# Batch 2's transposed q and k copied out by ScalarE and VectorE, its first k through another PSUM bank, its q and k loaded in halves of four heads

## The chip, the cores and the metric

The kernel runs on one core of one Trainium2 chip. The metric is the device time of one execution in microseconds (us). The kernel before takes 345.33 us, the median of three runs (345.21 to 345.88).

The engines are named as in the profile: PE is TensorE, PEld its weight loads, DVE is VectorE, ACT is ScalarE, POOL is GpSimd, SP is SyncE. Each engine works through its own queue in order. L254 is line 254 of the kernel before.

## The reference, cut to what matters

Inputs are `q`, `k`, `v` of 8 batches x 8 heads x 576 positions x 64, forget factors `f` of 8 x 8 x 576, and two weight matrices (512 x 2048 and 2048 x 512). For each batch and head a causal attention with decay is computed, and its output, 4608 tokens by 512, goes through a small MLP:

```
scores = q k^T / 8 + cum[i] - cum[j]        # cum = cumsum(log(clip(f, 1e-4, 1)))
attn   = softmax over j <= i
x      = (attn v), heads side by side       # 4608 x 512
h      = x w_in;  g = h - tanh(h);  out = g w_out
```

## The kernel before

Work is in fp16 with fp32 sums in PSUM. Heads are taken in pairs, four pairs to a batch. For the scores of a head both q and k must lie with the 64 head dimensions on the partitions (`QT` and `KT`, two buffers each, used by even and odd batches). How they get there depends on the batch. Batch 0 is turned by PE in blocks. **Batches 1 and 2** are loaded by POOL's DMA queue (`load_qk`, L213, with a cast from fp32 to fp16) and turned by PE, one pair at a time, in `trans` (L245). Batches 3 to 7 (`FAR = 3`) are turned by DMA.

`trans(b, c, src, dst, eng)` turns q or k of pair `c` of batch `b`: six PE transposes (L254) into one PSUM bank, then two copies to SBUF, one from partitions 0 to 63 into the even positions, one from partitions 64 to 127 into the odd ones. The two letters of `eng` name the engine of each copy: A is ACT (L261), V is DVE (L263).

The bank comes from a pool. `ps_tr` has one bank; `ps_m` has three, used in turn, and is shared with the MLP: a bank holds one tile of the first MLP product (`hps`, L448 or L462) until its gate is done, or one output tile of the second (`ops`, L581). `ps_sc` has two banks for scores (`ps`, L358), `ps_av` two for the attention output (`av`, L386).

The order on every engine is the order in which the program is written out (`manual_schedule`). The main loop is `slot(p, take)`, p = 4 to 32, one slot for each head pair from batch 1 on (p = 4 is batch 1's first pair, p = 8 batch 2's first). In slot p seven score tiles are emitted, each with its exponential on ACT (`e`, L367) and, from the second pair on, a causal mask on POOL (L377). Among them, by score tile number `ti`, come the loads listed in `LOADS`, the `values` of the pair before (L386, then three DVE operations L392 to L394), and the two `trans` calls for the next pair: q at `ti` 0 and k at `ti` 3, but at 2 and 4 in slot 7, which prepares batch 2's first pair. So batch 2 is turned in slots 7, 8, 9 and 10. Between these items MLP steps are spread: `mlp1` makes an `hps` tile, ACT takes its tanh (`th`, L414) and DVE adds it (`gt`, L415); `mlp2` adds four products to `ops` and copies it out on ACT (L585). `TAKE` says how many steps a slot gets: 5 in slot 7, 7 in slot 8, 9 in slot 9, 8 in slot 10.

The loads of batch 2's q and k are issued in slot 4, behind four loads of `wout` (L210), one DMA for all 8 heads of q at `ti` 5 and one for k at `ti` 6. POOL then issues, in the slots after, batch 2's v (L95, five DMAs in slot 6) and batch 3's q and k by heads (L106). Eight completion semaphores are used in turn by POOL's DMAs; a DMA waits until the one eight before it on the same semaphore has landed.

Of the kernel before, what the change touches and what calls it, by code (L numbers as in the profile page):

```python
# [22 lines left out]
def kernel(  # L23
# [13 lines left out]
    B, H, S, D = q.shape  # L37
# [4 lines left out]
    NPAIR = H // 2  # L42
# [34 lines left out]
    HH = H // 2  # L77
    raw = [[qkp.tile([P, RW], FP16, tag=f"{x}n{i}", name=f"{x}n{i}") for i in range(2)] for x in "qk"]
    qn, kn = ([t[0:S // NT6, :].rearrange("p (h n d) -> p h n d", h=H, n=NT6) for t in ts] for ts in raw)
# [8 lines left out]
    QT = [qkp.tile([D + 3, H, S], FP16, tag=f"QT{i}", name=f"QT{i}") for i in range(2)]  # L88
    KT = [qkp.tile([D + 3, H, PITCH], FP16, tag=f"KT{i}", name=f"KT{i}") for i in range(2)]
# [12 lines left out]
    def load_heads(dst, src, b, n):  # L102
        pn = min(P, S - n * P)
        to = dst[0:pn, n * P:n * P + D]
        to = bass.AP(to.tensor, to.offset, [list(to.ap[0]), [HP, H], [1, D]])
        nc.gpsimd.dma_start(out=to, in_=src[b, :, n * P:n * P + pn, :].rearrange("h p d -> p h d"))  # L106

    def turn_all(dst, src):
        nc.sync.dma_start_transpose(out=dst.rearrange("p (x t) -> p x t", t=P), in_=src[:, 0:TC])
# [5 lines left out]
    def load_v(b, n):  # L115
        load_block(vn[b % 2], v, b, n)

    def raw_of(b):
        return 1 if b == FAR else 0
# [48 lines left out]
    def load_aug(b):  # L168
        i, h0 = b % 2, b * H
        nc.sync.dma_start(out=KT[i][D:D + 1, :, 0:S], in_=chi[h0:h0 + H, :])  # L170
        nc.sync.dma_start(out=QT[i][D + 2:D + 3, :, :], in_=cq[h0:h0 + H, :])
        nc.sync.dma_start(out=KT[i][D + 1:D + 2, :, 0:S], in_=clo[h0:h0 + H, :])
# [40 lines left out]
    def load_qk(dst, src, b, h0, h1):  # L213
        nc.gpsimd.dma_start(
            out=dst[b % 2][:, h0:h1, :, :].rearrange("p h n d -> p h (n d)"),
            in_=src[b, h0:h1, :, :].rearrange("h (p n) d -> p h (n d)", n=NT6))

    LOADS = {(NPAIR, 5): [lambda: load_qk(qn, q, 2, 0, H)],
             (NPAIR, 6): [lambda: load_qk(kn, k, 2, 0, H)]}
    for i in range(2 * HF):  # L220
        LOADS.setdefault((2 * NPAIR + 3 + i // 4, i % 4 * 2), []).append(lambda i=i: weight_sums(i))
    for b in range(2, B):
        p0 = (b - 1) * NPAIR
        for n in range(NJ):
            LOADS.setdefault((p0 + (2 if b == 2 else 1), n), []).append(lambda b=b, n=n: load_v(b, n))
        LOADS.setdefault((p0, 0), []).append(lambda b=b: load_aug(b))
        if b < FAR:
            continue
        for n in range(NJ):
            LOADS.setdefault((p0 - 1, n), []).append(lambda b=b, n=n: load_heads(raw[0][raw_of(b)], q, b, n))  # L230
            LOADS.setdefault((p0, n), []).append(lambda b=b, n=n: load_heads(raw[1][raw_of(b)], k, b, n))
        LOADS.setdefault((p0, 4), []).append(lambda b=b: turn_all(TQ, raw[0][raw_of(b)]))
        LOADS.setdefault((p0 + 1, 4), []).append(lambda b=b: turn_all(TK, raw[1][raw_of(b)]))
# [4 lines left out]
    E, XN, GT, M2, AV = {}, {}, {}, {}, {}  # L238
# [5 lines left out]

    def trans(b, c, src, dst, eng):  # L245
        pn, g3 = S // NT6, NT6 // 2
        if b == 1 and src is kn:
            t32 = ps_m.tile([P, UW], FP32, tag="m", name="t32")
        else:
            t32 = ps_tr.tile([P, UW], FP32, tag="tr", name="t32")  # L250
        t16 = t32.bitcast(FP16)[:, 0:2 * S // 2].rearrange("p (a g n) -> p a g n", a=2, g=g3)
        for a in range(2):
            for g in range(g3):
                nc.tensor.transpose(out=t16[:, a, g, :],  # L254
                                    in_=src[b % 2][:, 2 * c + a, 2 * g:2 * g + 2, :],
                                    identity=id16[0:pn, 0:pn])
        for e in range(2):
            to = dst[b % 2][0:D, 2 * c:2 * c + 2, e:S:2].rearrange("d a (p g) -> d a p g", g=g3)
            of = t16[e * D:(e + 1) * D, :, :, :].rearrange("d a g p -> d a p g")
            if eng[e] == "A":  # L260
                nc.scalar.activation(out=to, in_=of, func=AF.Copy)  # L261
            else:
                nc.vector.tensor_copy(out=to, in_=of)  # L263
# [83 lines left out]
    def scores(b, c, ti):  # L347
        ps = ps_sc.tile([P, 512], FP32, tag="sc", name="ps")
        if ti == LAST:
            e = EL[(b * NPAIR + c) % 3]  # L350
        else:
            e = aex.tile([P, 512], FP16, tag="e", name="e")
        lo = min(x[4] for x in TILES[ti])
        hi = max(x[4] + x[3] for x in TILES[ti])
        for a, j, i0, n, col in TILES[ti]:
            h = 2 * c + a
            edge = min(P, n) if (b, c) == (1, 0) and i0 == j * P else 0
            nc.tensor.matmul(out=ps[:, col:col + n], lhsT=KT[b % 2][0:D + 3, h, j * P:(j + 1) * P],  # L358
                             rhs=QT[b % 2][0:D + 3, h, i0:i0 + n], start=True, stop=not edge)
            if edge:  # L360
                nc.tensor.matmul(out=ps[:, col:col + edge], lhsT=neg16, rhs=tri16[:, 0:edge],
                                 start=False, stop=True)
            for ib in range(j, NJ):
                w0 = min(ib * P, S - P)
                if i0 <= ib * P < i0 + n:
                    E[(b, h, j, ib)] = e[:, col + w0 - i0:col + w0 - i0 + P]
        nc.scalar.activation(out=e[:, lo:hi], in_=ps[:, lo:hi], func=AF.Exp, scale=qscale)  # L367
        if (b, c) == (1, 0):
            return
        col, cp, step, wd = MASKS[ti]  # L370
        view = e[:, col:col + (cp - 1) * step + wd]
        if cp == 1:
            pat = [[1, wd]]
        else:
            view = bass.AP(view.tensor, view.offset, [list(view.ap[0]), [step, cp], [1, wd]])
            pat = [[0, cp], [1, wd]]
        nc.gpsimd.affine_select(out=view, in_=view, compare_op=ALU.is_ge, fill=0.0,  # L377
                                base=0, pattern=pat, channel_multiplier=-1)
# [19 lines left out]
    def turn(b, c):  # L398
        xn = XN.pop((b, c))
        r0 = b % RB * S  # L400
        nc.sync.dma_start_transpose(out=XR[:, c, r0:r0 + S - D].rearrange("p (n t) -> p n t", t=P),
                                    in_=xn[:, 0:NJ - 1, :].rearrange("p n d -> p (n d)"))
        nc.sync.dma_start_transpose(out=XR[:, c, r0 + S - D:r0 + S], in_=xn[D:P, NJ - 1, :])
# [27 lines left out]
    def weight_sums(i):  # L431
        what, x = divmod(i, HF // 2)
        lo, hi = slice(2 * x, 2 * x + 2), slice(HF + 2 * x, HF + 2 * x + 2)
        b11, b12, b21, b22 = (wout[:, r, c] for r in (lo, hi) for c in (slice(0, HD), slice(HD, DM)))
        t2x = t2[x // 2][:, x % 2 * 2:x % 2 * 2 + 2, :]
        out, in0, in1 = ((t1[:, lo, :], b12, b11), (t2x, b22, t1[:, lo, :]),
                         (t3[:, lo, :], b22, b12), (tn4[:, lo, :], b21, t2x))[what]
        nc.vector.tensor_tensor(out=out, in0=in0, in1=in1, op=ALU.subtract)
# [167 lines left out]
    def att_items(p):  # L606
        items = []
        here = pairs[p] if p < len(pairs) else None
        before = pairs[p - 1] if NPAIR < p else None
        after = pairs[p + 1] if p + 1 < len(pairs) else None  # L610
        for ti in range(len(TILES)):
            if here:
                items.append((lambda ti=ti: scores(*here, ti), "s%d" % ti))
            for load in LOADS.get((p, ti), ()):
                items.append((load, ""))
            late = 2 * (p == 2 * NPAIR - 1)
            if ti == late and after and after[0] < FAR:
                items.append((lambda: trans(*after, qn, QT, "AV" if after[0] == 1 else "VV"), "q"))
            if ti == 1 and before:
                items.append((lambda: (values(*before), turn(*before)), "v"))  # L620
            if ti == 3 + late // 2 and after and after[0] < FAR:
                items.append((lambda: trans(*after, kn, KT, "VV"), "k"))
        return items

    goal = [0]
# [114 lines left out]
    scores0(4, 3)  # L740
    step()
    trans(1, 0, qn, QT, "AV")
    scores0(4, 4)
    turn0(3)
# [40 lines left out]
```

## Time and profile before

| what | value |
|---|---|
| median of 3 runs | 345.33 us (345.21 to 345.88) |
| profiled execution: time, and span of the core | 346.0 us, 344.3 us |
| granted TensorE clock | 1.00 |
| busy PE, DVE, ACT, POOL | 334.6, 236.2, 222.9, 158.6 us |
| PE transposes L254 (batches 1 and 2) | 96, 203 to 208 ns each |
| copies L263 on DVE | 27, 783 to 815 ns each |
| copies L261 on ACT | 5, 806 to 829 ns each |
| stretch 58 to 62 us, busy PE | 1.88 + 1.31 of 4.00 us |
| stretch 76 to 92 us, busy PE, DVE, ACT | 15.76, 13.81, 12.38 of 16.00 us |
| stretch 120 to 300 us, busy PE | 180.00 of 180.00 us |

The span is the time between the first and the last instruction on the core; the profiled time lies 1.7 us above it. A busy time adds up the durations of an engine's instructions. PE's instructions are pipelined, so the start of one matmul after the start of another tells more of PE's pace than their durations do.

### The profile page before, as it was taken

What the parts mean: (1) busy time and instruction counts of PE and PEld (TensorE: products, weight loads), DVE (VectorE), ACT (ScalarE), POOL (GpSimd) and SP (SyncE); (2) the same over time, 40 slices, a digit from 0 to 9 for tenths busy, and PEclk for the clock granted to TensorE, in tenths of its full rate; (3) what the DMA queues carried; (4) which work ended last, traced back from release to release, by engine and by line L of the source; (5) the groups of instructions that cost most, each with busy time, mean ns of one, the idle gap of its engine ahead of it and who ended that gap; (6) DMA issues with size and microseconds to landing.
All of it is one profiled execution on the core that took longest, in us unless ns stands there. A gap on an engine that the chain in (4) does not pass through costs nothing.

```text
span 344.3 us, 8688 instructions
## 1 busy us (share of the span) xinstructions
PE 334.6 (97%) x3354; PEld 235.2 (68%) x3354; DVE 236.2 (69%) x481; ACT 222.9 (65%) x417; POOL 158.6 (46%) x318
## 2 busy tenths in 40 slices
PE   7989999999999999999999999999999999999995
PEld 3879875655455557888886568656887786486485
DVE  6496886658953598558764895478637865975973
ACT  4677976558755786578757875687568844623631
POOL 8966448755267726664586548652222210000000
PEclk9999999999999999999999999999999999999999
DMA  9999999999799999999999999999330013002002
GB/s 88 140 197 188 204 203 141 169 159 233 126 141 127 202 175 151 123 193 184 164 145 188 172 159 181 182 172 184 91 110 19 17 50 109 3 30 93 0 32 91
DMA packets 161323, 45.96 MB, mean 134 GB/s; under 512 B 141506, under 2 KB 159234, under 8 KB 161282
## 3 DMA queue, kind: packets, MB, share of 16 engines
q0 software_dynamic: 100128, 18.36, 74.8%
q1 hardware_dynamic: 61074, 26.99, 39.8%
q8 instruction: 26, 0.43, 0.6%
q14 instruction: 15, 0.12, 0.1%
q10 hardware_dynamic: 80, 0.07, 0.1%
HBM read 36.85 MB, written 9.44 MB: 134 GB/s over the span
## 4 chain that ended last, share of the span: by engine, by line
PE 88%; DVE 5%; ACT 4%; POOL 1%; issue 1%; DMA 1%; ACTq 0%; DVEq 0%
PE hps L462 31%; PE cx L503 14%; PE cz L503 11%; PE ps L358 10%; PE ops L581 7%; PE av L386 7%; PE hps L448 2%; PE ps L300 2%; DVE gt L415 1%; PE t L272 1%; ACT e L305 1%; DVE QT L263 1%; ACT e L367 1%; ACT th L414 1%; PE av L313 1%
## 5 line engine op out<-in xcount | busy, mean ns | idle before, releaser
L415 DVE TENSOR_TENSOR gt<-hps,th 128x512 f16<-128x512 f32 x144 | 98.4, 688 | 42.7 <-ACT th L414 41.6
L462 PE MATMUL hps<-XR,win 128*128 128x512 f16 (+4 forms) x640 | 125.7, 336 | 0.2 <-DVE gt L415 0.2
L367 ACT ACTIVATE e<-ps 128x512 f16<-128x512 f32 x168 | 98.5, 594 | 37.4 <-PE ps L358 34.7
L414 ACT ACTIVATE th<-hps 128x512 f32<-128x512 f32 x144 | 86.1, 598 | 29.5 <-PE hps L462 19.8
L377 POOL TENSOR_SCALAR_AFFINE_SELECT e<-e 128x128 f16<-128x128 f16 x162 | 55.3, 342 | 105.9 <-ACT e L367 105.6
L462 PEld LDWEIGHTS <-win 128*128 128x128 f16 x640 | 56.3, 97 | 43.7 <-issue 0.5
L358 PE MATMUL ps<-QT,KT 67*128 67x512 f16 (+1 forms) x336 | 68.7, 277 | 0.5 <-DVE KT L263 0.3
L503 PEld LDWEIGHTS <-gt 128*128 128x128 f16 x560 | 52.5, 97 | 8.2 <-DVE gt L415 0.4
L358 PEld LDWEIGHTS <-KT 67*128 67x128 f16 x336 | 31.9, 98 | 21.7 <-DVE KT L263 0.8
L95 POOL DMA_DIRECT2D vn<-in_v_dram x40 | 34.2, 859 | 5.9 <-DMA win<-in_moe_w_in_dram 3.0
L581 PE MATMUL ops<-wout,gt 128*128 128x512 f16 x128 | 32.6, 378 | 0.0
L386 PEld LDWEIGHTS <-e 128*128 128x128 f16 x784 | 28.1, 97 | 3.3
L496 DVE TENSOR_TENSOR snap<-cz,snap 128x512 f32<-128x512 f32 x21 | 14.5, 691 | 22.4 <-PE cz L503 7.4
L386 PE MATMUL av<-vn,e 128*128 128x65 f16 x784 | 29.2, 193 | 0.0
L503 PE MATMUL cz<-wout,gt 128*128 128x256 f16 x224 | 27.8, 272 | 0.0
L394 DVE TENSOR_TENSOR xn<-av,rs 128x640 f16<-128x640 f32 x28 | 23.1, 825 | 1.0
L503 PEld LDWEIGHTS <-sw 128*128 128x128 f16 x224 | 21.1, 97 | 3.9
L106 POOL DMA_DIRECT2D qn<-in_q_dram x25 | 21.3, 852 | 1.7 <-issue 1.7
L106 POOL DMA_DIRECT2D kn<-in_k_dram x25 | 21.3, 853 | 1.2 <-issue 1.2
L540 ACT ACTIVATE snap<-cx 128x512 f32<-128x512 f32 (+1 forms) x16 | 8.7, 544 | 16.2 <-PE cx L503 16.2
L581 PEld LDWEIGHTS <-gt 128*128 128x128 f16 x128 | 11.2, 97 | 9.8
L305 ACT ACTIVATE e<-ps 128x512 f16<-128x512 f32 x25 | 14.3, 596 | 4.9 <-PE ps L303 2.9
(108 smaller groups left out, 377.4 us busy)
## 6 DMA issues: line engine op xcount, KB each, us to landing
vn<-in_v_dram POOLq DMA_DIRECT2D x32, 128.0 KB, 6.7
out_dram<-ost SPq DMA_DIRECT2D x14, 256.0 KB
out_dram<-snap SPq DMA_DIRECT2D x14, 256.0 KB
qn<-in_q_dram POOLq DMA_DIRECT2D x24, 128.0 KB, 5.3
kn<-in_k_dram POOLq DMA_DIRECT2D x24, 128.0 KB, 4.5
QT<-TQ SPq DMA_DIRECT2D x10, 288.0 KB
KT<-TK SPq DMA_DIRECT2D x10, 288.0 KB
win<-in_moe_w_in_dram POOLq DMA_DIRECT2D x2, 1024.0 KB, 12.1
```

The costliest lines, as they stand in the source:

```text
L95: nc.gpsimd.dma_start(out=dst[0:pn, n, h0:h1, 0:D], in_=src[b, h0:h1, n * P:n * P + pn, :].rearrange("h p d -> p h d"))
L106: nc.gpsimd.dma_start(out=to, in_=src[b, :, n * P:n * P + pn, :].rearrange("h p d -> p h d"))
L358: nc.tensor.matmul(out=ps[:, col:col + n], lhsT=KT[b % 2][0:D + 3, h, j * P:(j + 1) * P], rhs=QT[b % 2][0:D + 3, h, i0:i0 + n], start=True ...
L367: nc.scalar.activation(out=e[:, lo:hi], in_=ps[:, lo:hi], func=AF.Exp, scale=qscale)
L377: nc.gpsimd.affine_select(out=view, in_=view, compare_op=ALU.is_ge, fill=0.0, base=0, pattern=pat, channel_multiplier=-1)
L386: nc.tensor.matmul(out=av[:, a, ib, :], lhsT=E.pop((b, 2 * c + a, j, ib)), rhs=vn[b % 2][:, j, 2 * c + a, 0:D + 1], start=(j == 0), stop=( ...
L394: nc.vector.tensor_tensor(out=xn.rearrange("p i (a d) -> p a i d", a=2), in0=av[:, :, :, 0:D], in1=rs.to_broadcast([P, 2, NJ, D]), op=ALU. ...
L414: nc.scalar.activation(out=th, in_=hps, func=AF.Tanh, scale=-1.0)
L415: nc.vector.tensor_tensor(out=to, in0=view(hps), in1=view(th), op=ALU.add)
L462: nc.tensor.matmul(out=hps[:, o:o + n], lhsT=win[:, ci, ft * P:(ft + 1) * P], rhs=XR[:, ci, t:t + n], start=(ci == 0), stop=(ci == NCH - 1))
L503: nc.tensor.matmul(out=ps, lhsT=stationary(u, LHS[ph], ft, m), rhs=moving(RHS[ph], ft), start=fresh and ft == 0, stop=(ft == HF - 1), skip ...
L581: nc.tensor.matmul(out=ops, lhsT=GT[(u, ft, m)], rhs=wout[:, ft, :], start=(ft == 0), stop=(ft == NFT - 1))
```

## The change

Three things are done, all for batch 2 alone. In `trans`, the two copies of each of its eight transposed tiles (q and k of four pairs) go to ACT and DVE, where both went to DVE; batch 1's stay as they are (q by ACT and DVE; k by DVE alone but for its first pair). The k tile of batch 2's first pair takes a bank of `ps_m` where it took the bank of `ps_tr`; batch 1's k did so before. And batch 2's q and k are loaded in four DMAs, four heads each, in the order q low, k low, q high, k high, where they were loaded in two.

```diff
-    LOADS = {(NPAIR, 5): [lambda: load_qk(qn, q, 2, 0, H)],
-             (NPAIR, 6): [lambda: load_qk(kn, k, 2, 0, H)]}
+    LOADS = {(NPAIR, 5): [lambda: load_qk(qn, q, 2, 0, HH), lambda: load_qk(kn, k, 2, 0, HH)],
+             (NPAIR, 6): [lambda: load_qk(qn, q, 2, HH, H), lambda: load_qk(kn, k, 2, HH, H)]}
...
     def trans(b, c, src, dst, eng):
         pn, g3 = S // NT6, NT6 // 2
-        if b == 1 and src is kn:
+        if src is kn and (b, c) <= (2, 0):
             t32 = ps_m.tile([P, UW], FP32, tag="m", name="t32")
         else:
             t32 = ps_tr.tile([P, UW], FP32, tag="tr", name="t32")
...
             if ti == late and after and after[0] < FAR:
-                items.append((lambda: trans(*after, qn, QT, "AV" if after[0] == 1 else "VV"), "q"))
+                items.append((lambda: trans(*after, qn, QT, "AV"), "q"))
             if ti == 1 and before:
                 items.append((lambda: (values(*before), turn(*before)), "v"))
             if ti == 3 + late // 2 and after and after[0] < FAR:
-                items.append((lambda: trans(*after, kn, KT, "VV"), "k"))
+                items.append((lambda: trans(*after, kn, KT, "VV" if after[0] == 1 else "AV"), "k"))
```

## The prediction

> **What bounds the kernel now.** I read the page's totals and its chain first, then the waits around slots 7 to 10 (58 to 93 us), then that stretch in order of time.
>
> ```profile
> PE 334.6 (97%) x3354; PEld 235.2 (68%) x3354; DVE 236.2 (69%) x481; ACT 222.9 (65%) x417; POOL 158.6 (46%) x318
> ...
> PE 88%; DVE 5%; ACT 4%; POOL 1%; issue 1%; DMA 1%; ACTq 0%; DVEq 0%
> ```
>
> PE sets the end. It is busy 180.00 of 180.00 us from 120 to 300 us, so what is won before that stays won, and work on another engine is free unless PE comes to wait for it. The question is therefore where PE waits on batch 2's copies. The waits from 50 to 95 us:
>
> ```profile
> PE t L254 <- DVE QT L263: 0.8, 1, 0.8
> PEld L358 <- DVE KT L263: 0.8, 1, 0.8
> ...
> PE hps L462 <- DVE gt L415: 0.2, 1, 0.2
> ```
>
> The first is batch 2's first k, the third is touched below; the second (at 55 us) is batch 1's last k, which stays. The timeline of the first:
>
> ```profile
> 58.31 0.42 PE L254 MATMUL t<-id,qn 96*128 96x96 f16 x6
> ...
> 58.94 1.60 DVE L263 COPY QT<-t 64x576 f16<-64x576 f16 x2
> ...
> 59.49 0.38 PE L358 MATMUL ps<-QT,KT 67*128 67x512 f16 x1
> ...
> 60.69 0.42 PE L254 MATMUL t<-id,kn 96*128 96x96 f16 x6 [0.81 <-DVE QT L263]
> ...
> 60.94 1.04 PE L448 MATMUL hps<-XR,win 128*128 128x256 f16 x8
> ```
>
> q and k share the one `ps_tr` bank, so the k transposes stand until both q copies are done (60.54). PE issues a 512-column score in 0.22 us (the chain's time for it), so it could have gone on at 59.71: 0.98 us lost. The chain in order of time shows the second place:
>
> ```profile
> 78.41 0.61 ACT th L414
> 79.04 0.69 DVE gt L415
> 79.73 0.71 DVE KT L263
> 80.45 0.81 DVE KT L263
> ...
> 81.29 0.70 DVE gt L415
> ...
> 82.04 1.02 PE hps L462 x4
> ```
>
> A gate waits behind two k copies on DVE, and holds a `ps_m` bank that `hps` needs. The score before went at 81.50 and needs 0.22, so `hps` is 0.32 late. The same shape closes slot 10: score at 91.53, `hps` at 92.00, 0.25 late. In all 0.98 + 0.32 + 0.25 = 1.55 us hang on batch 2's copies.
>
> **The copies.** Eight of 0.80 us leave DVE, eight come to ACT. Rows of batch 1 have this pair already:
>
> ```profile
> 35.08 0.81 ACT L261 ACTIVATE QT<-t 64x576 f16<-64x576 f16 x1
> ...
> 35.74 0.58 ACT L367 ACTIVATE e<-ps 128x512 f16<-128x512 f32 x1
> ...
> 35.92 0.81 DVE L263 COPY QT<-t 64x576 f16<-64x576 f16 x1 [0.31 <-ACT QT L261]
> ```
>
> Two things to see. DVE starts when ACT has ended (35.89): the copies go one after the other, not at once, and in the changed program too every second copy waits for the first. A pair takes 0.81 + 0.03 + 0.80 = 1.64 where it took 1.60. So latency gains nothing; what is gained is that DVE is free for 0.8 us each time. And ACT starts its next work 0.66 after a copy's start, so a copy costs ACT's queue 0.66, not 0.81; by the same reading a tanh or an exponential costs some 0.50 when its input is ready (starts at 82.08, 82.57, 83.10, 83.59).
>
> The new wait is DVE's for ACT. Behind it stand gates and the norm of `values`; who waits for those is `hps`, by its bank. Behind the copy on ACT stand exponentials and tanhs, for which scores (two banks) and gates wait.
>
> **Slot 7, walked through.** ACT's q copy starts when the transposes end (58.73 + 0.04 = 58.77), ends 59.58; DVE's runs to 60.42. The k transposes no longer wait for either and go at 59.71; `hps` follows at 59.97 and ends at 61.01. ACT: exponential 59.97, k copy 60.47 to 61.28, tanh 61.13, exponential 61.63 to 62.24. DVE's k copy 61.32 to 62.12. PE meanwhile has issued four scores and an `ops` group and wants batch 2's first score at 62.15; it needs the k copy (62.16) and a score bank (that exponential, 62.28). It waits 0.13. Before, it went at 63.15, now at 62.28. Gain 0.87; the 0.13 is what takes the place of the 0.98.
>
> **The bank.** The k tile takes a turn of `ps_m`, so each later tile needs the bank of the tile one nearer to it. The next `hps` needs the gate of the one before last (ended 57.84, wanted 59.97); the one after needs the k copies (62.12, wanted 63.86); the next `ops` needs a gate that ends at 62.81 and is wanted at 65.8. Cost nothing; if ACT slipped by over 1.7 us there, the second would bind.
>
> **Slots 9 and 10.** Everything is 0.87 earlier. In slot 9 PE's k transposes end at 77.76; ACT, free of a tanh at 78.04, copies to 78.85 and ends the next tanh at 79.30; DVE copies 78.89 to 79.69 and ends the gate at 80.38. `hps` wants its bank at 80.85 (81.72 less 0.87): 0.4 to spare, the 0.32 goes. In slot 10 the same chain (ACT's copy 87.87 to 88.68, tanh to 89.13, DVE's copy to 89.52, gate to 90.21) meets a want of 90.56 (91.75 less 0.87 and 0.32): 0.3 to spare, the 0.25 goes. Slot 8's `trans` calls have 2 us or more: its MLP steps are `mlp2`, without gates.
>
> **The loads.** Twice two DMAs instead of two on POOL, at 0.70 us (the row of batch 1's 288 KB load) against 0.79 and 0.77: 1.2 us more at 38 us, with 3.25 us of idle POOL behind it before the mask at 41.83. The landings before:
>
> ```profile
> qn<-in_q_dram POOLq DMA_DIRECT2D x1, 576.0 KB, 18.0
> kn<-in_k_dram POOLq DMA_DIRECT2D x1, 576.0 KB, 20.6
> ```
>
> Issued at 37.02 and 37.80, q landed at 55.0, k at 58.4. Nobody waited: q is turned at 58.31, k could be at 59.71. In halves and in order: q low near 52.3 and k low near 55.0 (half and all of the bytes up to q's landing, counted from the last `wout` at 49.6), the high halves by 58.4. Gain nothing, as even all of k is there before 59.71. The two extra DMAs shift POOL's semaphore turns: the last v load (issued 54.50) now waits for q low, batch 3's first two q loads (56.91, 58.06) for k low and q high, the third (59.32) still for the rest of k. Margins 2.2, 1.9, 1.4 and 0.9: cost nothing, unless the rival below holds.
>
> [...]
>
> **Sum.** 0.98 - 0.13 + 0.32 + 0.25 = 1.42 us. Profiled span 344.3 to 342.9, profiled time 346.0 to 344.6; the median of the runs lies 0.67 under that time, so 345.33 - 1.42 = 343.9 us. A measurement tells 0.2% (0.7 us) from no change. Bounds: no new wait and 1.55 gained (343.8), or a second new wait like the first (344.1); the runs of before lie up to 0.55 above their median and 0.12 below it, so I add 0.3 on either side: 343.5 to 344.4.
>
> **Rival 1: ACT becomes late.** For: slot 10 holds eight tanhs, six exponentials and a short one; at their full 0.60, 0.59 and 0.28 plus two copies at 0.81 that is 10.2 us against a PE slot of 9.75 (82.90 to 92.65). Then ACT has no slack: in slot 7 the exponential ends at 62.57 and PE waits 0.46, and the gates in slots 9 and 10 come behind ACT's copies as late as they came behind DVE's. Gain 0.98 - 0.46 = 0.5: 344.8 us. Against: the 0.66 and 0.50 above, and 12.38 busy of 16 us from 76 to 92. Chance 0.13.
>
> **Rival 2: slower, by a load.** POOL's last v load now waits at 54.50 for q low, and behind it in POOL's queue stand two masks (55.19, 0.66 for both) that `values` at 56.32 needs. If the four halves share the queue and land together near 58.4, the masks end at 59.8 and PE waits about 3.3 us; less the 1.4 gained, 347.2 us. It decides when q low lands after about 55. Against: q landed 3.4 us before k though issued only 0.8 before, so the queue went in order. Chance 0.09.
>
> [...]
>
> **Rival 3: nothing shows.** PE gains in slot 7 and gives it back at a wait that comes earlier with it, such as batch 3's DMA-turned q and k. Before, PE waits for no DMA from 96 us on. 345.3 us, chance 0.08.
>
> **Numbers.** Forecast 0.70; rivals 0.13, 0.09, 0.08. Rival 1's 0.5 us lies under the 0.7 that can be told; I count 0.08 of its 0.13 as same and 0.05 as faster, for a part of the gates' gain that is kept. Faster 0.70 + 0.05 = 0.75, same 0.08 + 0.08 = 0.16, slower 0.09. The range takes the forecast and rival 1, with the same margin below and above: 343.4 to 345.0; rivals 2 and 3, 0.17, are left out.
>
> **What would show it.** Right: the k transposes follow the score in slot 7 at 0.22; batch 2's first score near 62.3; `hps` of slots 9 and 10 without a stop; 13 copies on ACT, 19 on DVE, each of batch 2's DVE copies behind an ACT one. Wrong: PE waits for ACT's exponentials in slots 9 and 10 (rival 1); POOL standing before a v load at 54 us with PE waiting on `values` (rival 2); a gap on PE after 96 us (rival 3).

## The result, and the profile after

The changed kernel takes 343.89 us (median of 20 runs, 342.94 to 345.69), the kernel before, run beside it, 345.75 (20 runs, 344.57 to 347.23). The ratio is 0.9953 [0.9940, 0.9966], a gain of about 1.6 us (1.2 to 2.1) where the sum said 1.42. By that ratio the 345.33 us shown at the start become 343.7, forecast 343.9. That 343.89 meets 343.9 so closely is luck: the kernel before took 0.42 us more here than in the three runs that the sum started from.

The page's totals and its shares of the chain, of the changed kernel:

```profile
PE 334.9 (98%) x3354; PEld 235.8 (69%) x3354; DVE 229.7 (67%) x473; ACT 227.4 (66%) x425; POOL 160.0 (47%) x320
...
PE 91%; DVE 4%; ACT 3%; DMA 1%; issue 0%; ACTq 0%; DVEq 0%
```

Eight instructions have left DVE (481 to 473) and come to ACT (417 to 425); L261 runs 13 times and L263 19 times. PE's own work is the same; its share of the chain rises because DVE and ACT hold it less. The waits from 50 to 95 us:

```profile
DVE QT L263 <- ACT QT L261: 6.0, 5, 3.2
DVE KT L263 <- ACT KT L261: 2.6, 3, 1.5
PEld L358 <- DVE KT L263: 1.1, 2, 0.8
```

The two waits that the prediction wanted gone, of the k transposes for `QT` and of `hps` for a gate, are no longer in this list. DVE's waits for ACT are the order of each pair of copies: they are long and cost nothing but the small part that reaches PE in the third line (0.8 of it is batch 1's last k, as before). Slot 7 in order of time:

```profile
58.92 0.42 PE L254 MATMUL t<-id,qn 96*128 96x96 f16 x6
59.38 0.81 ACT L261 ACTIVATE QT<-t 64x576 f16<-64x576 f16 x1 [0.47 <-PE t L254]
60.05 0.26 ACT L367 ACTIVATE el<-ps 128x128 f16<-128x128 f32 x1
60.10 0.38 PE L358 MATMUL ps<-QT,KT 67*128 67x512 f16 x1
...
60.22 0.81 DVE L263 COPY QT<-t 64x576 f16<-64x576 f16 x1 [0.59 <-ACT QT L261]
60.32 0.42 PE L254 MATMUL t<-id,kn 96*128 96x96 f16 x6
...
61.07 0.80 ACT L261 ACTIVATE KT<-t 64x576 f16<-64x576 f16 x1
...
61.73 0.58 ACT L414 ACTIVATE th<-hps 128x512 f32<-128x512 f32 x1
...
61.91 0.81 DVE L263 COPY KT<-t 64x576 f16<-64x576 f16 x1 [0.89 <-ACT KT L261]
...
62.85 0.38 PE L358 MATMUL ps<-QT,KT 67*128 67x512 f16 x1
```

The k transposes go 0.22 after the score, while DVE's q copy has only begun. Batch 2's first score (62.85) waits for the last k copy, which ends at 62.72. Slot 9, in the changed kernel, where a stop of 0.32 had been:

```profile
78.61 0.81 ACT L261 ACTIVATE KT<-t 64x576 f16<-64x576 f16 x1
...
79.47 0.81 DVE L263 COPY KT<-t 64x576 f16<-64x576 f16 x1
...
80.31 1.33 DVE L415 TENSOR_TENSOR gt<-hps,th 128x512 f16<-128x512 f32 x2
...
81.20 0.38 PE L358 MATMUL ps<-QT,KT 67*128 67x320 f16 x2
...
81.42 1.03 PE L462 MATMUL hps<-XR,win 128*128 128x512 f16 x4
```

**Starts must be compared from a common point.** The q transposes of slot 7 start at 58.92 where they had started at 58.31, and the profiled execution had fallen back by that 0.61 us long before any changed instruction: batch 1's first q transposes start at 30.24 instead of 29.63. It begins with batch 0. The same four transposes, before and after:

```profile
13.41 0.39 PE L272 MATMUL t<-id,qn 128*67 128x128 f16 x4
```

```profile
13.72 0.63 PE L272 MATMUL t<-id,qn 128*67 128x128 f16 x4
```

PE starts at half pace (groups of four transposes start 0.43 us apart and last 0.63) and turns to full pace (0.22 apart, 0.39) by 13.4 us in one execution and after 14 us in the other. So I take all times from the start of slot 7's q transposes. The table has, from PE's timelines, how long after it four points come: slot 7's k transposes, batch 2's first score, and the `hps` behind the 320-column score of slots 9 and 10 (in slot 10 the whole loss of batch 2's copies has been paid).

| kernel (q transposes of slot 7 at) | k transposes | first score | `hps` slot 9 | `hps` slot 10 |
|---|---|---|---|---|
| before (58.31) | 2.38 | 4.84 | 23.73 | 33.69 |
| changed (58.92) | 1.40 | 3.93 | 22.50 | 32.22 |
| bank alone (58.11) | 1.40 | 3.92 | 22.82 | 32.78 |
| copies alone (58.24) | 2.15 | 4.62 | 23.19 | 32.90 |
| halves alone (58.82) | 2.37 | 4.84 | 23.72 | 33.68 |
| bank and copies (57.44) | 1.40 | 3.93 | 22.51 | 32.22 |
| both copies on ACT (58.86) | 1.40 | 5.55 | 24.67 | 35.18 |

The changed kernel gains 33.69 - 32.22 = 1.47 us there, and its PE is busy in every microsecond from 76 to 300 us (16.00 of 16, 8.00 of 8, 20.00 of 20, 180.00 of 180), so the gain stays. PE's last sixteen matmuls, before and after:

```profile
338.82 1.91 PE L503 MATMUL cx<-tn,gt 128*128 128x256 f16 x16
```

```profile
337.98 1.91 PE L503 MATMUL cx<-tn,gt 128*128 128x256 f16 x16
```

They start 338.82 - 58.31 = 280.51 us after the common point before and 337.98 - 58.92 = 279.06 after it in the changed kernel, 1.45 earlier. The profiled span shrinks by less, 344.3 to 343.4, because of the later start (1.47 - 0.61 = 0.86).

### The profile page after: what moved, and what is told of

It is laid out like the page before. It is cut to its first block, busy times and chain, and to the rows that moved or that the text cites. A ratio compares the mean times of both kernels' runs of the same rounds, so it can differ in the third digit from the quotient of the medians.

```text
span 343.4 us, 8692 instructions
## 1 busy us (share of the span) xinstructions
PE 334.9 (98%) x3354; PEld 235.8 (69%) x3354; DVE 229.7 (67%) x473; ACT 227.4 (66%) x425; POOL 160.0 (47%) x320
## 4 chain that ended last, share of the span: by engine, by line
PE 91%; DVE 4%; ACT 3%; DMA 1%; issue 0%; ACTq 0%; DVEq 0%
PE hps L462 32%; PE cx L503 14%; PE ps L358 11%; PE cz L503 11%; PE ops L581 8%; PE av L386 7%; PE hps L448 3%; PE ps L300 2%; PE t L272 1%; ACT e L305 1%; DVE gt L415 1%; PE t L254 1%; PE av L313 1%; DMA snap<-in_f_dram 1%; DVE KT L263 1%; PE ps L303 1%
## 5 line engine op out<-in xcount | busy, mean ns | idle before, releaser
L377 POOL TENSOR_SCALAR_AFFINE_SELECT e<-e 128x128 f16<-128x128 f16 x162 | 55.6, 343 | 103.1 <-ACT e L367 102.0
L305 ACT ACTIVATE e<-ps 128x512 f16<-128x512 f32 x25 | 14.4, 596 | 5.4 <-PE ps L303 3.5
```

## The experiments

Each edit is told against the kernel before or the changed one; each ratio is to the kernel before, with its 95% interval. The kernel before was timed again beside them (345.56 us with the first four, 345.71 with the rest).

**The bank alone.** Against before:

```diff
-        if b == 1 and src is kn:
+        if src is kn and (b, c) <= (2, 0):
```

> Only the bank is changed: batch 2's first k in ps_m, copies both on VectorE, loads whole. Theory (PE waits in three places, each with its own cause): the k transposes of slot 7 follow the score before them at 0.22 us instead of 1.20; batch 2's first score is about 0.95 us earlier; the two late hps tiles of slots 9 and 10 (0.32 and 0.25) stay. Gain 0.95 us, 0.9972 of before. Rival (the copies on two engines make the gain, the bank is idle): 1.000. Rival (loads): 1.000.

Measured: 0.9975 [0.996, 0.999], 344.75 against 345.56 us. The k transposes go at 1.40, the first score at 3.92. The stops of slots 9 and 10 are there as before. From its timeline:

```profile
78.54 1.61 DVE L263 COPY KT<-t 64x576 f16<-64x576 f16 x2
...
80.18 2.11 DVE L415 TENSOR_TENSOR gt<-hps,th 128x512 f16<-128x512 f32 x3
...
80.39 0.38 PE L358 MATMUL ps<-QT,KT 67*128 67x320 f16 x2
...
80.93 1.02 PE L462 MATMUL hps<-XR,win 128*128 128x512 f16 x4
```

`hps` comes 0.54 after the score instead of 0.22: two k copies on DVE stand ahead of the gate, the first of the three here. So the bank is worth 33.69 - 32.78 = 0.91 us, and slot 7 needs no copy on ACT.

**The copies alone.** Against before:

```diff
-items.append((lambda: trans(*after, qn, QT, "AV" if after[0] == 1 else "VV"), "q"))
+items.append((lambda: trans(*after, qn, QT, "AV"), "q"))
-items.append((lambda: trans(*after, kn, KT, "VV"), "k"))
+items.append((lambda: trans(*after, kn, KT, "VV" if after[0] == 1 else "AV"), "k"))
```

> Only the engines of the copies are changed; batch 2's first k stays in ps_tr, loads whole. Theory: a pair on ScalarE and VectorE in turn is no quicker than two on VectorE, so the k transposes of slot 7 still wait for the q copies (0.86 instead of 0.98), while the gates of slots 9 and 10 no longer stand behind two copies and the two late hps tiles go. Gain 0.11 + 0.32 + 0.25 = 0.68 us, 0.998 of before. Rival (ScalarE becomes late): hps or scores of slots 9 and 10 wait for ScalarE, 1.000 to 1.002.

Measured: 0.9984 [0.9965, 1.0003], 345.21 against 345.56 us; the times alone don't show a gain. The trace does: 33.69 - 32.90 = 0.79 by slot 10, of which 0.57 are the two gates and 0.22 slot 7 (0.11 was expected there). ACT starts the first q copy while DVE is still at `xn`, so the q copies end 0.13 earlier, 2.10 after the q transposes' start instead of 2.23; the k transposes also follow them by 0.05 instead of 0.15, for a reason that is not shown. By PE's last matmuls 0.60 of the 0.79 is left (338.15 - 58.24 = 279.91 against 280.51); the rest goes near 148 us, where eight `hps` matmuls take 1.23 instead of 1.04, a loss whose cause is open. The k transposes of slot 7 still stand:

```profile
59.42 0.38 PE L358 MATMUL ps<-QT,KT 67*128 67x512 f16 x1
...
60.02 0.10 PEld L254 LDWEIGHTS <-kn 96*128 96x128 f16 x1 [0.72 <-DMA kn<-in_k_dram]
...
60.39 0.42 PE L254 MATMUL t<-id,kn 96*128 96x96 f16 x6 [0.59 <-DVE QT L263]
```

They wait for the bank, as expected, but in this execution their weights also waited for the load of k itself, in one piece, issued at 40.05 and landing 19.9 later. The prediction had given it 1.3 us to spare (58.4 against 59.71).

**The halves alone.** Against before:

```diff
-LOADS = {(NPAIR, 5): [lambda: load_qk(qn, q, 2, 0, H)],
-         (NPAIR, 6): [lambda: load_qk(kn, k, 2, 0, H)]}
+LOADS = {(NPAIR, 5): [lambda: load_qk(qn, q, 2, 0, HH), lambda: load_qk(kn, k, 2, 0, HH)],
+         (NPAIR, 6): [lambda: load_qk(qn, q, 2, HH, H), lambda: load_qk(kn, k, 2, HH, H)]}
```

> Only the loads are changed: four of four heads instead of two of eight. Theory: nobody waits for these loads, 1.000. Rival (the halves hold GpSimd's queue through its semaphores): slower, up to 3 us if q low lands after 55 us. Rival (the halves are what makes the k transposes early): 0.997.

Measured: 1.0014 [0.9996, 1.0032], 346.08 against 345.56 us; in the trace 33.68 against 33.69. By themselves they bring and cost nothing that shows. But the first link of rival 2 is there. POOL in this run:

```profile
55.76 0.69 POOL L95 DMA_DIRECT2D vn<-in_v_dram  x1 [0.68 <-DMA qn<-in_q_dram]
56.45 0.90 POOL L377 TENSOR_SCALAR_AFFINE_SELECT e<-e 128x128 f16<-128x128 f16 x3
```

q low landed at 55.5, and the last v load waited 0.68 for it with three masks behind. `values` (56.83) did not wait for them.

**Bank and copies, without the halves.** Against the changed kernel, the diff just shown turned round: the `-` lines in, the `+` lines out.

> The changed kernel with its loads whole again (bank and copies changed). Theory: as the changed kernel, 0.9955, with k landed about 1 us before the k transposes of slot 7 want it. Rival (the halves are needed once the bank lets the k transposes go early): they wait for k, a gain of 0.6 us or less, 0.998.

Measured: 0.9956 [0.994, 0.9973], 344.34 against 345.56 us; in the trace 32.22, the changed kernel's own number. So in these executions the gain is the bank's and the copies' alone. Their single gains, 0.91 + 0.79, are more than 1.47 because the 0.22 of slot 7 lies inside the bank's wait.

**Both copies on ACT.** Against the changed kernel, for batch 2:

```diff
-trans(*after, qn, QT, "AV")
+trans(*after, qn, QT, "AV" if after[0] == 1 else "AA")
-trans(*after, kn, KT, "VV" if after[0] == 1 else "AV")
+trans(*after, kn, KT, "VV" if after[0] == 1 else "AA")
```

> The changed kernel with both copies of batch 2's tiles on ScalarE. Theory (a copy takes 0.66 us of ScalarE's queue, a tanh or an exponential 0.50): in slot 7 batch 2's first score comes at 63.26 instead of 62.28 on the clock of before, which costs the slot's gain; slots 9 and 10 still have no late hps. Gain over before 0.45 us, 0.9987. Rival (ScalarE pays full durations): slot 10 needs 11.9 us of ScalarE in 9.75, at least 2 us slower than before, 1.006.

Measured: 1.0068 [1.0047, 1.0090], 348.00 against 345.71 us. My theory failed; the rival has the time. ACT in slot 7, with the score that waits for it:

```profile
59.31 1.63 ACT L261 ACTIVATE QT<-t 64x576 f16<-64x576 f16 x2 [0.47 <-PE t L254]
...
60.97 0.28 ACT L367 ACTIVATE el<-ps 128x128 f16<-128x128 f32 x1
...
61.62 1.62 ACT L261 ACTIVATE KT<-t 64x576 f16<-64x576 f16 x2
...
63.27 0.60 ACT L414 ACTIVATE th<-hps 128x512 f32<-128x512 f32 x1
...
63.77 1.72 ACT L367 ACTIVATE e<-ps 128x512 f16<-128x512 f32 x3
...
64.41 0.38 PE L358 MATMUL ps<-QT,KT 67*128 67x512 f16 x1 [1.38 <-ACT e L367]
```

The start to start of 0.66 that I had read for a copy holds where one copy stands alone among ACT's other work. A copy behind a copy starts only when the first has ended, and what follows the second, though it is an exponential or a tanh, starts only when the second has ended: in slot 7 the two take 1.62 to 1.63, and the next operation starts 1.65 to 1.66 after the first, where 1.32 had been counted. All eight pairs of this run are like that (0.83 to 0.85 from the second copy to the next start); why the second copy is not overlapped is not shown. So the score waits 1.38 for an exponential. The rival's mechanism is only half right: a tanh here is still followed after 0.49 (82.16 to 82.65), and slot 7, which the rival did not name, has more than half of the loss by slot 10 (5.55 - 3.93 = 1.62). By slot 10 the kernel is 35.18 - 32.22 = 2.96 us behind the changed one, and an `hps` later waits 0.8 for the DMA that brings `XR`: 3.8, against a difference of the ratios of 4.0.

**Loads of two heads.** Against the changed kernel, eight loads instead of four (q and k by turns, two heads each):

```diff
-LOADS = {(NPAIR, 5): [lambda: load_qk(qn, q, 2, 0, HH), lambda: load_qk(kn, k, 2, 0, HH)],
-         (NPAIR, 6): [lambda: load_qk(qn, q, 2, HH, H), lambda: load_qk(kn, k, 2, HH, H)]}
+LOADS = {(NPAIR, 5): [lambda h=h, n=n: load_qk((qn, kn)[n], (q, k)[n], 2, h, h + 2)
+                      for h in (0, 2) for n in range(2)],
+         (NPAIR, 6): [lambda h=h, n=n: load_qk((qn, kn)[n], (q, k)[n], 2, h, h + 2)
+                      for h in (4, 6) for n in range(2)]}
```

> The changed kernel with batch 2's q and k loaded in eight DMAs of two heads. Theory (GpSimd's DMAs wait on semaphores taken in turn, eight apart): the last of them waits until the fourth wout load has landed (about 49.6 us), GpSimd stands until then with the masks of slot 5 behind it (wanted from 41.8 on), and values at 49 us waits some 3 us: 1.5 to 2.5 us slower than before, 1.004 to 1.007. Rival (only the landing of the loads counts): as the changed kernel, 0.9955.

Measured: 1.0160 [1.0131, 1.0189], 350.62 against 345.71 us. The direction was foreseen, not the size. POOL in order of time (the lines behind the loads have numbers 2 higher in this kernel, so L379 is L377):

```profile
48.04 0.63 POOL L214 DMA_DIRECT2D qn<-in_q_dram  x1 [1.91 <-PE ps L360]
51.13 0.63 POOL L214 DMA_DIRECT2D kn<-in_k_dram  x1 [2.46 <-DMA wout<-in_moe_w_out_dram]
51.81 0.91 POOL L379 TENSOR_SCALAR_AFFINE_SELECT e<-e 128x128 f16<-128x128 f16 x3
```

The eighth load stands 2.46 for the landing that its semaphore needs, the masks behind it start at 51.81, and PE's `values` wait for them:

```profile
48.78 0.38 PE L360 MATMUL ps<-QT,KT 67*128 67x448 f16 x2
52.16 1.06 PE L388 MATMUL av<-vn,e 128*128 128x65 f16 x14 [2.99 <-POOL e L379]
...
54.37 1.90 PE L583 MATMUL ops<-wout,gt 128*128 128x512 f16 x4
```

This is rival 2's chain (a load held for a landing, masks behind it, PE behind them), made to happen a few loads earlier. The size is in the last line: four `ops` that last 1.03 elsewhere last 1.90. PE's clock fell after the idle stretch; columns are the stretch, its length, busy time and instructions of PE, PEld, DVE, ACT and POOL, then the granted clock, the share of the DMA engines and GB/s:

```profile
53.00:54.00 1.00, 0.86 (x18) 0.50 (x15) 0.00 (x0) 0.00 (x0) 1.00 (x4) 1.00 1.31 196
54.00:55.00 1.00, 1.00 (x12) 0.65 (x11) 0.37 (x2) 0.00 (x0) 0.99 (x3) 0.51 0.82 124
55.00:56.00 1.00, 1.00 (x3) 0.30 (x2) 0.84 (x2) 0.00 (x0) 1.00 (x2) 0.50 0.48 56
56.00:57.00 1.00, 1.00 (x7) 0.71 (x6) 0.00 (x0) 0.28 (x1) 0.10 (x1) 0.50 1.81 119
57.00:58.00 1.00, 1.00 (x11) 0.82 (x9) 0.00 (x0) 0.49 (x2) 0.60 (x2) 0.79 0.96 66
```

From the q transposes of that slot to its k transposes PE needs 57.88 - 47.66 = 10.22 us where the changed kernel needs 52.51 - 48.25 = 4.26: 5.96 lost, 3.16 before `values` and 2.80 from its start on, of which the clock is some (0.49 + 0.50 + 0.50 + 0.21) = 1.70. The other 1.1 lies inside `values`, which take 2.21 us instead of 0.90 (0.18 of that is the clock) while POOL is still making their masks, until 54.08.

**The k of slot 6 one score earlier.** Against the changed kernel, to take away the wait for batch 1's last k that both kernels have:

```diff
-if ti == 3 + late // 2 and after and after[0] < FAR:
+if ti == 3 + late // 2 - (p == 2 * NPAIR - 2) and after and after[0] < FAR:
```

> The changed kernel with the k transposes of slot 6 (batch 1's last pair) one score tile earlier, before the hps tile of that slot. Theory: the wait for batch 1's last k copies (first score of slot 7, PE and PEld together about 0.5 us in start times) goes, as the two copies end near 53.3 instead of 54.9 on the clock of before. Gain 0.45 us over the changed kernel, 0.994 of before. Rival (the gate that now stands behind the copies holds hps): as the changed kernel, 0.9955.

Measured: 0.9963 [0.9942, 0.9984], 344.15 against 345.71 us: inconclusive, no gain over the changed kernel shows. In its profiled execution the wait did go: the first score of slot 7 starts 0.86 after the `ops` before it (55.19 - 54.33), in the changed kernel 1.31 (55.60 - 54.29). But PE waited for loads instead, batch 1's q (0.7) and `wout`:

```profile
54.33 1.02 PE L581 MATMUL ops<-wout,gt 128*128 128x512 f16 x4 [0.47 <-DMA wout<-in_moe_w_out_dram]
```

The last `wout` was issued at 38.21 there, 35.64 in the profile of before, and PE was 0.66 ahead of it (batch 1's first q transposes at 28.97 instead of 29.63). PE's lead alone does not bring these waits: in the run without halves it is larger (28.77), the last `wout` was issued at 35.99, and no load was waited for. Why the loads were late is not shown. Whether the earlier k would gain in an execution whose loads come in time is open.

**All of batch 1's k by ACT and DVE too.** Against the changed kernel:

```diff
-trans(*after, kn, KT, "VV" if after[0] == 1 else "AV")
+trans(*after, kn, KT, "AV")
```

> The changed kernel with batch 1's k copies on ScalarE and VectorE too. Theory: VectorE's first copy no longer stands behind a gate at the end of slot 6, the pair ends about 0.2 us earlier; slots 4 and 5 are tight on ScalarE (8.7 busy of 10 us), so a gain of 0.2 at most, 0.995 to 0.9955 of before. Rival (ScalarE late in slots 4 to 6): slower than the changed kernel by 0.5 us or more, 0.997.

Measured: 0.9967 [0.9948, 0.9985], 344.75 against 345.71 us, the same as the changed kernel within the intervals. Between 30 and 60 us the waits of PE's weights for `KT` shrink from 0.9 to 0.2 us, and PE's waits for an exponential grow instead, from 0.2 to 0.5; from batch 1's first q transposes to slot 7's it takes 28.82 us, the changed kernel 28.68. None of these versions beats the changed kernel.

## Why the prediction was right, and where it was not

**The first k.** Right. 0.98 was to go and 0.13 to come back, 0.85 in the sum (0.87 by the times of the walk); the first score comes 4.84 - 3.93 = 0.91 earlier. The new wait is about 0.10. The steps hold too, not only the size: set back by 0.61, ACT's k copy starts at 60.46 (60.47 in the walk), DVE's at 61.30 (61.32) and the score at 62.24 (62.28). The bank alone does it, in line with the prediction's reading that a pair on two engines is no quicker (1.64 against 1.60; in the changed kernel 59.38 to 61.03, 1.65).

**The two gates.** Right: 0.32 and 0.25 forecast; the `hps` distances show (23.73 - 22.50) - 0.91 = 0.32 and 1.47 - 1.23 = 0.24. The bank alone leaves both, the copies alone remove both.

**ACT, rival 1.** It did not come, but my reason against it was too wide. 0.66 for a copy is true in the changed kernel, where each stands alone among exponentials and tanhs (59.38 to 60.05, 61.07 to 61.73); read as the price of a copy anywhere it is wrong, as both copies on ACT show.

**The loads, rival 2.** Costed at nothing, and right for the times. q low was to land near 52.3; it was issued at 37.77 and took 15.2, so 53.0, with the execution 0.6 late. The halves did not land together, as rival 2 needs, but in the order of their issue, at 53.0, 54.1, 55.5 and 57.2. The runs show no cost of the two more DMAs: from the landing of the last `wout`, the last half takes 6.6 to 7.8 us in the five runs with halves, and all of k 5.9 to 8.7 in the four with whole loads. What failed is the margins. I took 0.9 to 2.2 us from one execution, but the last `wout` is issued anywhere from 35.64 to 38.21 us in the profiled runs, in the copies-alone run k landed after it was wanted, and in the halves-alone run the margin of 2.2 us for q low was a wait of 0.68. The masks' chain is real (loads of two heads); with four halves only its first link showed, and PE waited for none of it. Halves do bring the first pair's k earlier when the loads are late: with the last `wout` issued at 37.6 in both, k low landed at 56.7 in the halves-alone run and all of k at 60.0 in the copies-alone one. What that is worth in time no comparison shows.

**Rival 3.** PE does not give the gain back: no wait takes its place after 92 us, and 1.45 us of it is there at the last matmuls.

**Size.** The sum, 1.42, and the trace, 1.47, differ by the first score (0.91 for 0.85), less 0.01 at the gate of slot 10. The 1.6 of the ratio lies above both, inside its interval (1.2 to 2.1).

## What to carry to other kernels

When a single buffer stands between a producer and two slow consumers, a second buffer may remove the whole wait (0.91 us here); moving half of the consumers' work to another engine then pays only where the queue that it leaves held something PE needs (the two gates here, 0.57 us). Compare two traces from a landmark just before the change, not from the start: here the start differed by 0.6 us, over a third of the gain. Before a queue is given more DMAs, ask what stands behind them when they must wait for a semaphore; the price can be more than the wait: here a load stood 2.46 us and PE 2.99, and PE ran at half pace (granted clock 0.50) for 3.4 us soon after, for a reason that is not shown.

## What the runs showed that I had not expected

**PE's pace at the start differs from run to run.** The next four transposes of batch 0 after those shown start at 13.38 us in the run without halves and at 14.85 in the changed kernel, batch 1's first q transposes at 28.77 and 30.24: 1.47 us both times. The two profiled executions took 343.65 and 345.12 us, again 1.47 apart, though from slot 7 on the two kernels agree to 0.01 us. So the pace at the start moves the time of a whole execution as much as this change does, and only many runs show the change in the times. The granted clock in the profile's rows is 1.00 before and behind the turn, as the trace's clock records begin only with it (at 12.99 us before, 14.41 in the changed kernel); only the durations (0.63, then 0.39 for four transposes) tell.

**PE's clock can fall in the middle, and a long pause is not needed.** In the run with loads of two heads PE stood 2.99 us, worked for 1.85 us at 1.00 and then for 3.4 us at 0.50 (1.70 lost at half pace). But in the run with all of batch 1's k by ACT and DVE the clock fell too, near the start, though PE never stood for more than 0.69 us at a time after its first matmul. Transposes of batch 0 in that run, four at a time:

```profile
6.91 0.39 PE L272 MATMUL t<-id,qn 128*67 128x128 f16 x4
...
9.53 0.63 PE L272 MATMUL t<-id,qn 128*67 128x128 f16 x4
...
12.53 0.39 PE L272 MATMUL t<-id,qn 128*67 128x128 f16 x4
```

The two falls are of about one length: in the second run the mean granted clock, 0.995 over 342.1 us, loses some 1.7 us too, or 3.4 us at half pace. What decides a turn is not shown. Before and in the changed kernel PE works from 1.87 us on and comes to full pace only at 12.99 and 14.41 us, with pauses of 0.3 us at most up to then; in nine of the ten executions full pace comes at 9.9 to 14.4 us, in the run with all of batch 1's k by ACT and DVE before 6.7.

**What a copy costs ACT depends on its neighbours.** 64x576 copies from PSUM: 0.66 to the next start for one copy that an exponential or a tanh follows; for two in a row 0.82 to the second and 0.83 from the second to whatever follows.
